# Layer two of a routed two-layer network: the second token halves of six experts with W2 held and h streamed

## The chip, the core and the metric

The kernel runs on one core of a Trainium2 chip. The core has five engines that each follow their own instruction queue: TensorE (PE in the profile; its weight loads are shown apart as PEld), VectorE (DVE), ScalarE (ACT), GpSimd (POOL) and SyncE (SP), which here only issues transfers. They wait for one another through semaphores. The metric is the device time of one execution in microseconds (us). Before the change three runs took 569.81, 570.81 and 574.17 us, a median of 570.81 us.

## The reference, cut to what matters

```
kv   = einsum('bhsd,bhse->bhde', k, v)            # 8 batches, 8 heads, 576 tokens, 64 wide
out  = einsum('bhsd,bhde->bhse', q, kv)
x    = (out / rms(out) * g_norm)  -> (8, 576, 512)
e    = expert of each token (argmax of logits, or the previous token's, by a local gate)
h    = max(x @ w1[e], 0)                          # 512 -> 1024
out  = softmax(logits)[e] * (h @ w2[e])           # 1024 -> 512, all in float32
```

There are 4608 tokens and 8 experts, and each token goes through one expert alone. With these inputs expert 0 has 455 tokens, and the others, sorted by load, have 720, 666, 605, 596, 588, 548 and 430.

## The kernel before, in words

The first part (the first 120 us or so) computes the attention part, writes the rows of x to a scratch tensor `xs` in DRAM and sorts the tokens into slots, expert by expert. Then expert 0 is computed, and after it the seven other experts one after the other, in order of their load: **ranks** 1 to 7, with room for WIDTHS = 720, 672, 608, 608, 592, 576 and 448 tokens. Rank 1's first matmul starts at 180.50 us of the profiled span; from there to the end is the part in which the change lies.

A rank is done in two token **halves**: `parts` (L1404) gives the first half 384 tokens (ranks 1 and 2) or 256, and the second half what is left: 336, 288, 352, 352, 336, 320 and 192. Each half has these stages:

- **Gathers.** The tokens' rows come from `xs` by indirect transfers that GpSimd issues: four for a block of 128 tokens, 128 quarter rows each (L785). `Block.scale` multiplies them by their gate on VectorE (L1339 to L1346), and `turn4` (L796) turns them, so that features lie on partitions: a 32x32 transpose on VectorE (L802), a copy on ScalarE (L806), a subtraction on VectorE (L807).
- **Layer one**, `first_wide` (L1053). Float32 precision is reached with two float32r parts of each number, a high one and a low one, and three matmuls for each product: high by high, low by high, high by low (`split_mm`, L960). W1 is the operand held in the array (stationary), and the tokens are streamed (moving), so a matmul streams as many columns as the half has tokens; there are 8 groups `f` of 128 hidden features x 4 pieces of the input x 3 = 96 matmuls. After each `f` ScalarE writes the high part of h (L1050) and VectorE the low part (L1051). Three PSUM banks take turns.
- **Layer two**, `Block.second` and `products` (L985 to L1017). Here each block of 128 tokens is done by itself: h is stationary, and W2 is moving, 512 columns: 8 x 3 = 24 matmuls of 512 columns for a block, whether it holds 128 tokens or 80. A last block of 32 or 64 tokens has its low parts put beside its high parts in the array, and takes 16 matmuls (`halves`, L1025 to L1040); layer one's `halved=True` prepares that (L1070). ScalarE copies the result from PSUM to the tile `ot` (L1013), and GpSimd issues one indirect transfer that scatters up to 128 whole rows of 2 KB to the output (L1016).

So second halves have three blocks, of 128+128+80, 128+128+32, 128+128+96, 128+128+96, 128+128+80 and 128+128+64 tokens: 72, 64, 72, 72, 72 and 64 matmuls of 512 columns.

The order of the instructions on PE, ACT, DVE and POOL in this part is the order of the code. Work for other engines is put between matmuls: `then` runs a step behind a group `f` of layer one, hooks run at an `f` of layer two, and `tick` (L1432) issues from two lists: `outs`, which is empty in the kernel before, and `todo`, the gathers for the half after the next. The weights of the next rank come in through SyncE, and `wsplit` splits them into high and low parts on ScalarE (L235, L238) and VectorE (L236, L239).

A function `second_turned` (L1367) stands in the file and is not called.

## Time and profile before

| What | us |
|---|---|
| three runs | 569.81, 570.81, 574.17 (median 570.81) |
| the profiled execution, its own time | 576.47 |
| its span, first to last instruction | 574.6 |
| mean granted TensorE clock in it | 0.992 of 2.4 GHz |
| PE busy | 548.0 (95%) |
| PEld, DVE, ACT, POOL busy | 481.5, 306.1, 238.5, 242.2 |

The profile is of one execution, 5.7 us above the median of the runs and 2.3 us above the slowest of them. "Busy" adds up the instructions of an engine; matmuls are pipelined, so one that starts every 0.23 us lasts 0.39 us in the rows, and the time a stage costs is read from the starts of its matmuls, not from their length. "issue" and "remote" behind an arrow stand for a wait that the profile can't put down to an instruction of another engine.

### The profile page before, as it was taken

Reading aid. Unit: us, or ns where it says so; the run is one execution under the profiler, and the core shown is the slowest. Engines: PE = TensorE matmul, PEld = TensorE weight load, DVE = VectorE, ACT = ScalarE, POOL = GpSimd, SP = SyncE. Lnnn points to the kernel's source line nnn. Section 1 sums busy time; section 2 is a strip of 40 time slices with the busy share of each in tenths; the row PEclk is TensorE's granted clock in tenths of the full one; section 3 lists DMA queues with packets and bytes.
Section 4 is the critical chain, followed back from the end, with each engine's and each line's share of the span. In section 5 each row is a group of like instructions: output and inputs, shape, how many; then the busy total and the mean of one; then the engine's idle time right before and its main releaser. Section 6 shows DMA issues by size and latency. Waiting matters only on the chain. (4 is left out here: it accounts for less than half of the span.)

```text
span 574.6 us, 11830 instructions
## 1 busy us (share of the span) xinstructions
PE 548.0 (95%) x4637; PEld 481.5 (84%) x4637; DVE 306.1 (53%) x638; ACT 238.5 (41%) x449; POOL 242.2 (42%) x305
## 2 busy tenths in 40 slices
PE   2999998989998999999989999999999999999996
PEld 2888887879877989798877998889897979898894
DVE  1125786669686724635435744474546554564610
ACT  1578886761254334331424341533433332434311
POOL 5234433251335736633352463366435744562001
PEclk9999998989999999999999999999999999999998
DMA  7999999970666345232441353445143533442010
GB/s 224 311 361 353 359 336 351 329 267 23 228 231 245 115 142 167 68 123 86 135 120 56 135 175 74 125 150 177 39 164 130 169 94 133 139 123 80 1 38 31
DMA packets 41296, 94.91 MB, mean 165 GB/s; under 512 B 7167, under 2 KB 7167, under 8 KB 41232
## 3 DMA queue, kind: packets, MB, share of 16 engines
q1 hardware_dynamic: 32032, 72.64, 37.2%
q0 software_dynamic: 7664, 21.41, 12.5%
q8 instruction: 38, 0.62, 0.5%
q10 hardware_dynamic: 1536, 0.02, 0.1%
q14 instruction: 26, 0.21, 0.1%
HBM read 73.85 MB, written 20.46 MB: 164 GB/s over the span
## 5 line engine op out<-in xcount | busy, mean ns | idle before, releaser
L785 POOL DMA_INDIRECT xr<-xs,gid x120 | 136.9, 1141 | 36.6 <-issue 35.4
L1051 DVE SCALAR_TENSOR_TENSOR hl<-ph,hh 128x512 fp32r<-128x512 f32 (+4 forms) x92 | 50.3, 548 | 126.9 <-ACT hh L1050 100.6
L1050 ACT ACTIVATE hh<-ph 128x512 fp32r<-128x512 f32 (+5 forms) x92 | 45.3, 496 | 143.8 <-PE ph L972 106.7
L1016 POOL DMA_INDIRECT out_dram<-ot,sidr x33 | 36.6, 1108 | 152.7 <-ACT ot L1013 90.7
L465 PE MATMUL po<-kvz,qT 128*64 128x146 f32 x512 | 45.6, 307 | 0.5 <-ACT kvz L434 0.4
L500 POOL TENSOR_TENSOR sq<-raw 128x576 f32<-128x576 f32 x16 | 20.4, 1276 | 55.0 <-ACT raw L469 38.0
L465 PEld LDWEIGHTS po<-kvz,qT 128*64 128x64 f32 x512 | 35.7, 145 | 6.3 <-issue 2.2
L1013 ACT COPY ot<-py 128x512 f32<-128x512 f32 (+2 forms) x33 | 19.2, 580 | 51.7 <-issue 31.7
L505 DVE TENSOR_REDUCE ms<-sq 128x9 f32<-128x576 f32 x32 | 23.1, 748 | 23.8 <-POOL sq L500 22.2
L380 PE MATMUL po<-vt,kt 64*64 64x64 f32 x1152 | 23.4, 233 | 10.7 <-DMA vt<-in_v_dram 10.7
L380 PEld LDWEIGHTS po<-vt,kt 64*64 64x64 f32 x1152 | 20.8, 145 | 14.2 <-issue 6.8
L469 ACT COPY raw<-po 128x876 f32<-128x876 f32 (+1 forms) x32 | 22.8, 715 | 13.8 <-PE po L465 13.6
L404 POOL COPY kvz<-kvp 64x128 f32<-64x128 f32 x64 | 20.3, 317 | 13.4 <-ACT kvp L384 8.7
L1346 DVE TENSOR_TENSOR xr<-xr,r 128x512 f32<-128x512 f32 x36 | 25.0, 696 | 1.2
L806 ACT CAST yh<-xT 128x512 fp32r<-128x512 f32 x17 | 10.6, 621 | 29.5 <-DVE xT L802 25.3
L802 DVE STREAM_TRANSPOSE xT<-xr 128x512 f32<-128x512 f32 x30 | 21.2, 708 | 0.6
L972 PE MATMUL py<-w_0h,hl 128*128 128x512 f32 (+2 forms) x54 | 21.3, 394 | 0.3 <-issue 0.3
L966 PE MATMUL py<-w_0h,hh 128*128 128x512 f32 (+2 forms) x54 | 21.3, 395 | 0.2 <-ACT ot L1013 0.2
L966 PE MATMUL py<-w_1h,hh 128*128 128x512 f32 (+2 forms) x54 | 21.4, 397 | 0.0
L971 PE MATMUL py<-w_0l,hh 128*128 128x512 f32 (+2 forms) x54 | 21.2, 392 | 0.0
L972 PE MATMUL py<-w_1h,hl 128*128 128x512 f32 (+2 forms) x54 | 21.1, 391 | 0.0
L971 PE MATMUL py<-w_1l,hh 128*128 128x512 f32 (+2 forms) x54 | 21.1, 390 | 0.0
(434 smaller groups left out, 1649.8 us busy)
## 6 DMA issues: line engine op xcount, KB each, us to landing
wst<-in_moe_w_dram SPq DMA_DIRECT2D x64, 512.0 KB
xs<-raw SPq DMA_DIRECT2D x36, 292.0 KB
kt<-in_k_dram SPq DMA_DIRECT2D x32, 288.0 KB
vt<-in_v_dram SPq DMA_DIRECT2D x32, 288.0 KB
qt<-in_q_dram SPq DMA_DIRECT2D x32, 288.0 KB
xr<-xs,gid POOLq DMA_INDIRECT x120
out_dram<-ot,sidr POOLq DMA_INDIRECT x36
xr<-xs,gidr POOLq DMA_INDIRECT x6
```

Of the source, the lines that this page charges most:

```text
L380: nc.tensor.matmul(pk[half(x ^ b), x, 0:D], ks[b][half(x), cd], vs[b][half(x), cd], start=(c == 0), stop=(c == C - 1))
L465: nc.tensor.matmul(po[half(b), x, o:o + n], lw[:, half(x)], kvb[:, z0:z0 + n], start=True, stop=True)
L469: nc.scalar.copy(cols[:, c0:c1].rearrange("p c (x e) -> p x c e", x=2), po[:, :, 0:(c1 - c0) * HW].rearrange("p x (c e) -> p x c e", e=HW))
L505: nc.vector.tensor_reduce(mss[g][:, :, 2 * n + x], sqs.pop((s, x)), axis=AX.X, op=ALU.add)
L785: i = nc.gpsimd.indirect_dma_start(out=xr[:, u * PW:(u + 1) * PW], out_offset=None, in_=xs.rearrange("t (q w) -> (t q) w", w=PW), in_offse ...
L966: mm = nc.tensor.matmul(ps, ah, bh, start=(first and i == 0), stop=False)
L971: nc.tensor.matmul(ps, ah, bl, start=False, stop=False)
L972: nc.tensor.matmul(ps, al, bh, start=False, stop=(last and i == n - 1))
L1016: return nc.gpsimd.indirect_dma_start(out=outf, out_offset=bass.IndirectOffsetOnAxis(ap=idx[0:m], axis=0), in_=ot[0:m], in_offset=None, bo ...
L1050: nc.scalar.activation(hh, ps, AF.Relu)
L1051: nc.vector.scalar_tensor_tensor(hl, ps[:, :, 0:nl], 0.0, hh[:, :, 0:nl].bitcast(F32), op0=ALU.max, op1=ALU.subtract)
L1346: nc.vector.tensor_mul(xv, xv, r4.unsqueeze(3).to_broadcast([P, NP, 2, D]))
```

## The change

In ranks 1 to 6 the second half's layer two is done by `second_turned`. For each of 4 groups `j` of 128 output features and each of 8 groups `f` of hidden features it holds a 128x128 piece of W2 and streams h, with as many columns as the half has tokens: 4 x 8 x 3 = 96 matmuls for all tokens of the half. VectorE then takes each of the 4 results out of PSUM with a 32x32 transpose into a quarter of one buffer `oq`, in which a partition holds, for a group `u` of 32 tokens, a quarter row of 128 features. One indirect transfer for each `u` scatters 128 quarter rows of 512 bytes, by the indices `sid4`, which are new. The scatters are put into `outs`, and `tick` issues three of them at a time, ahead of the gathers, in the next rank's first half; gathers then come two at a time in first halves and one in second halves.

What goes with it: W2's columns are put into another order when it is split, for ranks 1 to 6, so that the first halves, which still go block by block, read W2 in four runs of 128 columns and write `ot` in runs of 32 (`turned=True`); layer one of ranks 1 to 6 has no `halved` form; rank 6 has room for 560 tokens in the place of 576, so its second half has 304; `ot` has 2 buffers in the place of 3, and the turned tokens of expert 0's last blocks 1 in the place of 2; `by_quarter` computes `sid4` with some more small VectorE operations, and GpSimd writes one more constant, `spot`, at the start.

The transfers of SyncE stay as they were, in the same order. The changed order on the other engines, at three places:

PE, rank 3, from the end of layer one of the second half (`ph`, 352 tokens) to layer one of the next rank (256 tokens); `py` is layer two, `w_0` to `w_3` are tiles of W2 there, `h` and `l` at a name's end the high and low part. Before (the first seven of 72 matmuls in `py`):

```order
L972 MATMUL ph<-yh,w_7l 128x352
L966 MATMUL py<-w_0h,hh 128x512
L971 MATMUL py<-w_0l,hh 128x512
L972 MATMUL py<-w_0h,hl 128x512
L966 MATMUL py<-w_0h,hh 128x512
L971 MATMUL py<-w_0l,hh 128x512
L972 MATMUL py<-w_0h,hl 128x512
L966 MATMUL py<-w_1h,hh 128x512
```

And in the changed kernel:

```order
L987 MATMUL ph<-yh,w_7l 128x352
L981 MATMUL py<-hh,w_0h 128x352
L986 MATMUL py<-hl,w_0h 128x352
L987 MATMUL py<-hh,w_0l 128x352
L981 MATMUL py<-hh,w_0h 128x352
L986 MATMUL py<-hl,w_0h 128x352
```

72 matmuls of 512 columns have become 96 of 352, and all 8 groups of h are read by the first 24 of them, as they were by the first block's 24 before.

POOL, from the gathers for rank 3's second half on, through rank 3 and up to the scatters of its second half. Before (`xr` are gathers, `out_dram` scatters):

```order
L785 DMA xr<-xs,gid_88 128x146 x10
L1016 DMA out_dram<-ot,sidr 4608x512
L785 DMA xr<-xs,gid_88 128x146 x2
L1016 DMA out_dram<-ot,sidr 4608x512
L1040 DMA out_dram<-ot,sidr 4608x512
L785 DMA xr<-xs,gid_88 128x146 x6
L1016 DMA out_dram<-ot,sidr 4608x512
L785 DMA xr<-xs,gid_88 128x146 x2
L1016 DMA out_dram<-ot,sidr 4608x512
L785 DMA xr<-xs,gid_88 128x146 x10
```

And in the changed kernel:

```order
L800 DMA xr<-xs,gid_88 128x146 x12
L1380 DMA out_dram<-oq,sid_90 18432x128 x9
L800 DMA xr<-xs,gid_88 128x146 x6
L1031 DMA out_dram<-ot,sidr 4608x512
L800 DMA xr<-xs,gid_88 128x146 x2
L1031 DMA out_dram<-ot,sidr 4608x512
L800 DMA xr<-xs,gid_88 128x146 x12
L1380 DMA out_dram<-oq,sid_90 18432x128 x11
L800 DMA xr<-xs,gid_88 128x146 x4
```

Three scatters of whole rows have become 9 to 11 scatters of quarter rows, which stand in one piece ahead of the next rank's gathers.

DVE, rank 3, from the last low part of h in the second half to the next rank's first one (`xT`, `xl` are the next rank's tokens, `w_..l` weights to be split). Before:

```order
L1051 SCALAR_TENSOR_TENSOR hl<-ph,hh 128x352
L1339 TENSOR_TENSOR gs<-xr,oneh 128x28
...
L1346 TENSOR_TENSOR xr<-xr,r_4828 128x4x128
L802 STREAM_TRANSPOSE xT<-xr 128x4x4x32
L807 TENSOR_TENSOR xl<-xT,xh 128x4x128
L802 STREAM_TRANSPOSE xT<-xr 128x4x4x32
L807 TENSOR_TENSOR xl<-xT,xh 128x4x128
L239 SCALAR_TENSOR_TENSOR w_3l<-wst,gq,w_3h 128x1024
L236 TENSOR_TENSOR w_4l<-wst,w_4h 128x1024
L236 TENSOR_TENSOR w_5l<-wst,w_5h 128x1024
L1051 SCALAR_TENSOR_TENSOR hl<-ph,hh 128x2x256
```

And in the changed kernel:

```order
L817 STREAM_TRANSPOSE xT<-xr 128x4x4x32
L822 TENSOR_TENSOR xl<-xT,xh 128x4x128
L244 SCALAR_TENSOR_TENSOR w_3l<-wst,gq,w_3h 128x1024
L1407 STREAM_TRANSPOSE oq<-py 128x11x32
L817 STREAM_TRANSPOSE xT<-xr 128x4x4x32
L822 TENSOR_TENSOR xl<-xT,xh 128x4x128
L241 TENSOR_TENSOR w_4l<-wst,w_4h 128x1024
L1407 STREAM_TRANSPOSE oq<-py 128x11x32
L241 TENSOR_TENSOR w_5l<-wst,w_5h 128x1024
L1407 STREAM_TRANSPOSE oq<-py 128x11x32 x2
L1066 SCALAR_TENSOR_TENSOR hl<-ph,hh 128x2x256
```

Four transposes out of PSUM have come into the queue; what else stands there is as it was, with the two turns a little further apart.

The diff, cut to its core:

```diff
@@ -56,7 +56,7 @@
-    WIDTHS = (720, 672, 608, 608, 592, 576, 448)
+    WIDTHS = (720, 672, 608, 608, 592, 560, 448)
     NR = E - 1
@@ -110,6 +110,7 @@
     quart = const.tile([P, 2], F32, name="quart")
+    sid4 = const.tile([P, NP, NR * KBM - KBM], I32, name="sid4")
     own4 = const.tile([P, NP], F32, name="own4")
@@ -127,6 +128,10 @@
+    spot = const.tile([P, 1], F32, name="spot")
+    for n in range(NP):
+        nc.gpsimd.iota(spot[n * QD:(n + 1) * QD], pattern=[[0, 1]], base=0, channel_multiplier=1,
+                       allow_small_or_imprecise_dtypes=True)
     def floor_div(dst, src, n, tmp):
@@ -252,7 +257,7 @@
         hi, lo = (wtile(pool, nm + x) for x in "hl")
-        low_ = split_w(hi, lo, t, i, e > 1, False)
+        low_ = split_w(hi, lo, t, i, e > 1, 0 < e < E - 1)
         wt[e, i] = (hi, lo)
@@ -654,13 +659,23 @@
-        n = NR * KBM - KBM
+        n = NR * KBM
         pq4 = rbank[:, 128:128 + NP * n].rearrange("p (u n) -> p u n", n=n)
         for u in range(NP):
-            nc.tensor.matmul(pq4[:, u], sel[0][:, u], trs[0][:, KBM:], start=True, stop=True)
+            nc.tensor.matmul(pq4[:, u], sel[0][:, u], trs[0], start=True, stop=True)
         t = sm.tile([P, NP, n], F32, name="q4", tag="co")
         nc.vector.tensor_scalar(t, pq4, float(NP), quart[:, 1:2], op0=ALU.mult, op1=ALU.add)
-        nc.vector.tensor_scalar(gid4, t, quart[:, 0:1], None, op0=ALU.max)
+        nc.vector.tensor_scalar(gid4, t[:, :, KBM:], quart[:, 0:1], None, op0=ALU.max)
+        m = n - KBM
+        none = sm.tile([P, NP, m], F32, name="none", tag="lo")
+        nc.vector.tensor_scalar(none, pq4[:, :, 0:m], 0.0, None, op0=ALU.is_equal)
+        for i, w_ in enumerate(WIDTHS[:-1]):
+            if w_ % QD:
+                cell = none[:, w_ % P // QD, i * KBM + w_ // P:i * KBM + w_ // P + 1]
+                nc.vector.scalar_tensor_tensor(cell, spot, float(w_ % QD), cell,
+                                               op0=ALU.is_ge, op1=ALU.max)
+        nc.vector.scalar_tensor_tensor(sid4, none, float(NP * (NT + 1)), t[:, :, 0:m],
+                                       op0=ALU.mult, op1=ALU.add)
@@ -1117,7 +1132,7 @@
     def xtiles(pool, n, nm):
-        return tuple(pool.tile([P, ND, n], F32R, name=nm + x, bufs=2 if nm == "t" else 1)
+        return tuple(pool.tile([P, ND, n], F32R, name=nm + x, bufs=1)
                      for x in "hl")
@@ -1138,7 +1153,6 @@
         fourth.append(gather(xtile0(), cidx(gidx, 3)))
-        fourth.extend(xtiles(z, P, "t"))
@@ -1193,6 +1207,7 @@
                     assert "y" in done
+                    fourth.extend(xtiles(z, P, "t"))
                     turn(*fourth, 0, ps_t)
@@ -1353,18 +1368,24 @@
             return (products if last else second)(z, w, hh, hl, t0, None, cidx(sidr, self.c), ps_y, hooks,
-                                                   m=self.m, turned=False)
+                                                   m=self.m, turned=self.r < E - 1)
...
-    def brought(ys, x, bl):
-
-        m = -(-bl.m // QD) * QD
-        ot = z.tile([P, DM], F32, name="ot", bufs=ot_bufs[0])
-        fetch(ot[0:m], ys[x * P:x * P + m])
-        return ot
-
-    def second_turned(w, hh, hl, n, lot, hooks, sites):
+    out4 = out.rearrange("b s (q w) -> (b s q) w", w=P)
+    scattered = []
+
+    def scatter(oq, u, c):
+
+        i = nc.gpsimd.indirect_dma_start(
+            out=out4, out_offset=bass.IndirectOffsetOnAxis(
+                ap=sid4[:, u % NP, c + u // NP:c + u // NP + 1], axis=0),
+            in_=oq[:, u], in_offset=None, bounds_check=NT * NP - 1, oob_is_err=False)
+        for j in scattered:
+            tc.declare_no_dep(i.ins, j.ins.name, reason="a token is in one slot alone")
+        scattered.append(i)
+
+    def second_turned(w, hh, hl, n, c, hooks):
@@ -1385,21 +1406,7 @@
                                 py[:, 0:nu * QD].rearrange("p (u k) -> p u k", k=QD))
-        ys = dram.tile([HM, DM], F32, name="ys", bufs=2)
-        for q_ in range(NP):
-            fetch(ys[0:nu * QD, q_ * P:(q_ + 1) * P].rearrange("(u k) w -> k u w", k=QD),
-                  oq[q_ * QD:(q_ + 1) * QD, 0:nu])
-        ots = []
-
-        def scatter(x):
-            bl = lot[x]
-            nc.gpsimd.indirect_dma_start(
-                out=outf, out_offset=bass.IndirectOffsetOnAxis(ap=cidx(sidr, bl.c)[0:bl.m], axis=0),
-                in_=ots[x][0:bl.m], in_offset=None, bounds_check=NT - 1, oob_is_err=False)
-
-        outs.extend(lambda: None for _ in range(sites))
-        outs.append(lambda: ots.extend(brought(ys, x, bl) for x, bl in enumerate(lot)))
-        outs.extend(lambda x=x: scatter(x) for x in range(len(lot)))
+        outs.extend(lambda u=u: scatter(oq, u, c) for u in range(nu))
@@ -1426,14 +1433,17 @@
     z = wpool("z")
-    ot_bufs[0] = 3
+    ot_bufs[0] = 2
     todo = []
...
-        for lot in (outs, todo):
+        lot, n = (outs, 3) if outs else (todo, rate[0])
+        for _ in range(n):
             if lot:
                 lot.pop(0)()
+
+    rate = [1]
@@ -1463,6 +1473,7 @@
             todo = [what for bl in ma for what in bl.gathers()]
+            rate[0] = 2
             own = [lambda j=j: wsplit(*j)
@@ -1474,7 +1485,7 @@
             first_wide({i: wt[r, i] for i in range(NW1)}, hh, hl, *xt, n=na, then=then, each=tick,
-                       halved=True)
+                       halved=r == E - 1)
             w = {i: wt[r, i] for i in range(NW1 + NW2)}
@@ -1502,17 +1513,16 @@
             todo = [what for bl in mb_ for what in bl.gathers()]
+            rate[0] = 1
             first_wide(w, hh, hl, *yt, n=nb, then=then, each=tick,
-                       halved=True)
+                       halved=r == E - 1)
             xt = xtiles(xp, HM, "x")
             turns = [lambda x=x, bl=bl: bl.turn(*xt, x * P) for x, bl in enumerate(ma)]
-            pairs_ = list(enumerate(lb))
-            for left_, (x, bl) in zip(range(len(lb), 0, -1), pairs_ if ma else reversed(pairs_)):
+            if r < E - 1:
+                second_turned(w, hh, hl, nb, lb[0].c, spread(turns, nxt))
+            for x, bl in reversed(list(enumerate(lb)) if r == E - 1 else []):
+                left_ = x + 1
                 hooks = []
-                for f in (1, 4):
-                    two(hooks, f, turns)
-                if nxt:
-                    hooks.append((7, nxt.pop(0)))
                 end = bl.second(w, hh, hl, x * P, with_ticks(hooks), not ma and left_ == 1)
...
                 tick()
```

## Rows read from the trace of the kernel before

**Rows 1.** The page: busy share of PE, and its granted clock in 40 slices.

```profile
PE 548.0 (95%) x4637; PEld 481.5 (84%) x4637; DVE 306.1 (53%) x638; ACT 238.5 (41%) x449; POOL 242.2 (42%) x305
...
PEclk9999998989999999999999999999999999999998
```

**Rows 2.** Waits of PE from 255 to 575 us: total, times, longest.

```profile
PE ph L966 <- DVE hh L1070: 1.2, 1, 1.2
PE py L972 <- DVE hl L1051: 0.7, 1, 0.7
PE ph L971 <- DVE yl L807: 0.3, 1, 0.3
```

**Rows 3.** Stretches: length, then PE, PEld, DVE, ACT, POOL busy; clock, DMA.

```profile
216.04:230.77 14.73, 14.73 (x97) 14.73 (x96) 7.64 (x17) 5.83 (x10) 9.45 (x8) 1.00 0.52 160
230.77:247.36 16.59, 16.59 (x74) 12.57 (x73) 8.78 (x14) 5.28 (x8) 9.69 (x8) 1.00 0.30 75
281.00:295.28 14.28, 13.03 (x97) 12.83 (x96) 5.25 (x13) 5.14 (x9) 9.51 (x9) 1.00 0.62 188
295.28:311.43 16.15, 15.33 (x67) 10.86 (x65) 8.76 (x20) 4.83 (x8) 4.88 (x5) 1.00 0.12 30
333.63:349.10 15.47, 15.47 (x97) 15.47 (x96) 5.49 (x9) 5.34 (x9) 11.05 (x11) 1.00 0.63 188
349.10:366.37 17.27, 17.06 (x73) 12.65 (x73) 9.78 (x17) 6.08 (x9) 5.84 (x6) 1.00 0.25 67
388.76:403.97 15.21, 15.21 (x97) 15.20 (x96) 6.44 (x12) 5.92 (x10) 10.02 (x10) 1.00 0.58 176
403.97:420.57 16.60, 16.60 (x75) 12.90 (x74) 8.87 (x14) 5.71 (x8) 6.85 (x7) 1.00 0.25 76
443.17:458.58 15.41, 15.10 (x97) 14.87 (x97) 8.55 (x15) 6.72 (x11) 12.36 (x11) 1.00 0.61 180
458.58:475.20 16.62, 16.62 (x74) 12.56 (x73) 8.69 (x13) 5.70 (x8) 7.42 (x7) 1.00 0.35 99
497.42:511.58 14.16, 14.16 (x98) 14.05 (x96) 8.06 (x21) 6.00 (x11) 11.41 (x10) 1.00 0.57 174
511.58:526.13 14.55, 14.55 (x66) 12.02 (x65) 8.81 (x14) 5.69 (x8) 3.65 (x4) 1.00 0.25 71
```

**Rows 4.** Timeline of PE at rank 2's layer one: start, length, what.

```profile
281.00 0.30 PE L966 MATMUL ph<-yh,w_0h 128*128 128x288 f32 x1
281.13 0.29 PE L971 MATMUL ph<-yl,w_0h 128*128 128x288 f32 x1
```

**Rows 5.** DVE from 225 to 575 us, grouped: busy and mean ns.

```profile
L802 DVE STREAM_TRANSPOSE xT<-xr 128x512 f32<-128x512 f32 x30 | 21.2, 708 | 0.6
...
L1051 DVE SCALAR_TENSOR_TENSOR hl<-ph,hh 128x352 fp32r<-128x352 f32 x16 | 8.3, 523 | 22.4 <-issue 15.2 <-ACT hh L1050 7.2
```

**Rows 6.** The page: ScalarE copies out of PSUM, contiguous and interleaved.

```profile
L1013 ACT COPY ot<-py 128x512 f32<-128x512 f32 (+2 forms) x33 | 19.2, 580 | 51.7 <-issue 31.7
...
L469 ACT COPY raw<-po 128x876 f32<-128x876 f32 (+1 forms) x32 | 22.8, 715 | 13.8 <-PE po L465 13.6
```

**Rows 7.** POOL from 240 to 576 us, grouped: busy and mean ns.

```profile
L785 POOL DMA_INDIRECT xr<-xs,gid x98 | 107.8, 1100 | 29.9 <-issue 29.0 <-DVE hl L1051 0.3 <-DMA out_dram<-ot,sidr 0.3
L1016 POOL DMA_INDIRECT out_dram<-ot,sidr x29 | 31.5, 1087 | 136.4 <-ACT ot L1013 82.2 <-issue 23.0 <-DMA out_dram<-ot,sidr 13.1
```

**Rows 8.** Timeline of POOL, two gathers in a row.

```profile
292.85 1.00 POOL L785 DMA_INDIRECT xr<-xs,gid  x1 [0.30 <-issue]
294.15 1.00 POOL L785 DMA_INDIRECT xr<-xs,gid  x1 [0.30 <-issue]
```

**Rows 9.** Timelines of ACT and DVE, late parts of h, ranks 2 and 4.

```profile
298.95 0.71 ACT L1050 ACTIVATE hh<-ph 128x288 fp32r<-128x288 f32 x2 [3.86 <-remote]
301.07 0.42 DVE L1051 SCALAR_TENSOR_TENSOR hl<-ph,hh 128x256 fp32r<-128x256 f32 x1
407.31 0.53 DVE L1051 SCALAR_TENSOR_TENSOR hl<-ph,hh 128x352 fp32r<-128x352 f32 x1 [2.55 <-issue]
```

## The prediction, as it was written before the run

> **What bounds the kernel now.** The page comes first: PE is busy 95% of the span and its granted clock stands at the upper level, 2.4 GHz, in nearly all slices, while VectorE, ScalarE and GpSimd are busy for 53, 41 and 42% [rows 1]. The chain of waits does not help here, since most of it is "issue"; the table of waits of PE does: in the 320 us from 255 us on PE waits for other engines for little more than 2 us [rows 2]. So in this part time is matmul time, and a change is worth what it takes from PE's stream, as long as nothing new makes PE wait. The stretches [rows 3] cut this stream at the first matmul of each stage: the rows come in pairs, layer one and layer two of the second half, for ranks 1 to 6 in turn. PE is busy for the whole of most of them.
>
> **What a matmul costs.** Two neighbours of 288 columns start 0.13 us apart [rows 4], and layer one's 96 matmuls at 352 columns take 15.21 us [rows 3], 0.1584 us each. 288 columns at 2.4 GHz are 0.120 us and 352 are 0.1467, so each matmul carries some 12 to 14 ns beyond its columns. A 512-column matmul of layer two takes 16.60 / 72 = 0.2306 us (rank 4), or 14.55 / 64 = 0.2273 us (rank 6), where its columns are 0.2133.
>
> **The main term.** The new layer two is, in shape, a copy of layer one of the same half: 96 matmuls, W held, n columns streamed. So layer one's own stretch gives its price, and the gain is the difference within each pair of rows 3, both taken without waits:
>
> - Rank 1: 16.59 before. Layer one's 96 matmuls at 336 columns take 14.73. The first group of columns is 352 wide in 12 of the 96, 12 x 16 / 2.4 ns = 0.08. After: 14.81, gain 1.78.
> - Rank 2: 64 matmuls at rank 6's 0.2273 are 14.55; 96 at 0.1333 are 12.80. Gain 1.75.
> - Ranks 3 and 4: 16.60 to 15.21, gain 1.39 each.
> - Rank 5: 16.62 to 14.81, gain 1.81.
> - Rank 6: 14.55 before; 14.16 at 320 columns less 96 x 6.7 ns for 16 columns fewer, and 0.08 more for the first group, is 13.60 at 304. Gain 0.95, and layer one of this half gains 0.56 in the same way.
> - Layer one of ranks 1 and 5 has the wider first group too: 0.08 lost, twice.
>
> The sum is a gain of 9.47 us. The columns saved alone are worth more: some 23,500 in layer two, 9.8 us at 2.4 GHz, and 160 more matmuls at 13 ns take 2.1 back; rank 6's layer one gives the rest.
>
> A rule can be set against the row here. The Trainium skill, "TensorE: Matmul & The Clock Gate", section "Back-to-back issue gap", puts the gap between isolated matmuls at N/2.4 plus about 2.5 ns. By that the extra matmuls would cost 0.4 us and the gain would be some 11 us. These traces show 12 to 14 ns instead, and the sum stays with the rows.
>
> **What lies beside PE.**
>
> - VectorE gets 24 transposes out of PSUM of 288 to 352 columns. The nearest rows are 523 ns for a 352-column operation out of PSUM and 708 ns for a 512-column transpose [rows 5], so about 0.53 us each and 2.1 us in a second half. In rank 4's layer two VectorE is busy for 8.87 of 16.60 us; it becomes 11.0 of 15.2. Each has a PSUM buffer of its own to run in, and PE comes back to that buffer one group `j`, some 3.7 us, later. Hidden. The few operations for `sid4` and the constant `spot` are short, on engines that wait there anyway: nothing.
> - ScalarE loses three copies of 580 ns in each of these halves.
> - Runs of 32 in the place of whole rows: ScalarE's copy of 876 columns with interleaved output takes 715 ns against 580 for 512 contiguous ones [rows 6], no price for the pattern; the 512-column transpose reads and writes in runs of 32 and takes what plain operations take. So splitting W2 and writing `ot` cost what they did.
> - GpSimd: 9 to 11 scatters for 3. One takes 1.09 us, as a gather of quarter rows does [rows 7], and two gathers in a row start 1.30 us apart [rows 8]. With rank 3's 11 scatters, 8 gathers for rank 4's first half, 2 scatters of whole rows and 12 gathers, rank 4 holds 33 issues, 42.9 us; its PE time would be 22.39 (from 366.37 to 388.76) + 15.21 + 15.21 = 52.8. The gathers that are needed first stand behind the 11 scatters: issued by 11 + 4 + 1 + 4 issues, 26 us after the rank's start, while their use comes in group 6 of the next layer one, at about 22.4 + 6 x 1.9 = 34 us. Some 8 us of room, for landing too. Hidden.
> - The reordered W2 is streamed in four runs of 128 columns in the first halves: 14 blocks x 24 = 336 matmuls. No row shows such an operand on PE. Nothing points to a gain, so the lower end is 0; the upper end is one matmul's own extra, 13 ns, for each of three further runs, 39 ns or 13 us in all. I take 0, by ScalarE's rows, where interleaving is free.
>
> **Waits at the seams.** Layer two used to read the last part of h after 22 of its 0.23 us matmuls, 5.1 us after its start; now it comes there after 22 x 0.158 = 3.5 us (352 columns) or 2.9 (288). ScalarE's last parts of h are sometimes late, by waits that the profile names "remote": in rank 4 the low part is ready at 407.31 + 0.53 = 407.84, 3.87 us after layer two's start, and in rank 2 at 301.49, 6.2 us after it [rows 9]. If these delays come again in the same places, rank 4 loses 0.4 us and rank 2 loses 3.3 where it loses 1.6 now: a gain of 9.47 becomes 1.78 + 0.05 + 1.39 + 0.99 + 1.81 + 0.95 + 0.56 - 0.16 = 7.4. If none of today's waits returns (1.60 and 14.28 - 12.80 = 1.48 in rank 2, 17.27 - 16.60 = 0.67 in rank 3, 15.41 - 14.73 = 0.68 in rank 5's layer one), it is 13.9. I take the middle way, 9.5.
>
> **From the profile to the runs.** The profiled execution took 576.5 us, which would give 567.0; it stands 5.7 above the median of the runs. The stages lie inside it and should be as long in the other runs, so from the median 570.8 the forecast is 561.3.
>
> **The rivals.**
>
> 1. *The gain is eaten at the seams.* PE reaches h earlier in every second half, and ScalarE's delays are 3 to 5 us long. For it: two of six halves had one within reach [rows 9], and VectorE's queue between two groups `j` is fuller. Against it: PE hardly waits today. If four more halves lost 1 to 1.5 us on top of the 7.4 case, 2 or 3 us of gain are left: about 568.
> 2. *The streamed runs cost.* At 39 ns for each of 336 matmuls 13.1 us are lost: 570.8 - 9.5 + 13.1 = 574.4. It decides from 28 ns on. Against it: ScalarE's and VectorE's rows; on PE no row speaks.
> 3. *GpSimd becomes the bound: slower.* Rank 4 has room for 11 scatters of (52.8 - 22 x 1.30) / 11 = 2.2 us. Were each to cost 3.0 us, start to start, rank 4 would last 61.6 in the place of 52.8, and by the same count ranks 2, 3, 5 and 6 would last 3.7, 3.0, 9.4 and 7.0 us more: 32 us in all, 593. For it: they are many, and stand ahead of the gathers in one queue. Against it: 98 gathers of the same 128 pieces average 1.10 us [rows 7] with VectorE busy beside them, and the issue order shows no scatter of this kind waiting for the one before. The Trainium skill, "SBUF — State Buffer", section "SBUF: two separate sides", would make such issues wait whenever a VectorE operation holds the port that it shares with GpSimd; the gathers' rows show no such stretch.
>
> That the change does not do what it says is ruled out by the order of the instructions: 96 matmuls and 9 to 11 scatters stand there.
>
> **The numbers.** Chances: the forecast 0.66 (its own range 557 to 565: gains of 13.9 and 7.4, and the runs' spread), the first rival 0.19, the second 0.05, the third 0.06, something unforeseen on the slow side 0.04. A measurement of this kernel tells about 1%, 5.7 us, from no change: below 565.1 is faster. Nearly all of the forecast and a tenth of the first rival lie there: 0.67. Within 1% lie the rest of these, and most of the second rival: 0.22. Slower: 0.11. The range reaches from 556 to 571, over the first rival, and leaves out the other two.
>
> **What would show it.** Right: layer two of ranks 1 to 6 with 96 matmuls 0.133 to 0.16 us apart, as in layer one of the same half; first halves as long as before (22.2 to 22.6 us in ranks 3 to 5); GpSimd's scatters 1.3 us apart. Wrong: 512-column matmuls of the first halves over 0.25 us apart (rival 2); scatters over 2 us apart and VectorE's scaling waiting for gathers (rival 3); waits of PE for `hh` or `hl` at the first group `j` (rival 1).

## The result: 1.2 to 1.7% faster

The changed kernel took 565.65 us (median of 567.41, 560.20, 563.89 and 568.47), the kernel before 571.74 in four runs: a ratio of 0.9875 [0.9829, 0.9921]. Two later measurements put it at 0.9842 [0.9797, 0.9888], 563.38 us, and 0.9835 [0.9801, 0.987], 562.83 us, each against the kernel before on the same chip (571.77 and 571.89). So the medians gain 6.1, 8.4 and 9.1 us. The forecast was 561.3 us, 0.983 of the 570.81 it started from.

The page after, in the lines that answer [rows 1], and those of the new operations (line, engine, operation, count | busy us, mean ns | idle time before it, by what):

```profile
PE 536.9 (95%) x4797; PEld 493.9 (87%) x4797; DVE 314.4 (56%) x649; ACT 229.5 (41%) x431; POOL 293.6 (52%) x354
...
L1380 POOL DMA_INDIRECT out_dram<-oq,sid x63 | 67.9, 1077 | 56.8 <-DVE oq L1407 39.4
...
L1407 DVE STREAM_TRANSPOSE oq<-py 128x352 f32<-128x352 f32 (+2 forms) x24 | 12.6, 526 | 17.6 <-PE py L987 17.4
```

160 more matmuls, 11 us less of PE; GpSimd is the engine that pays, 242 to 294 us. The stretches after, in the order of [rows 3] (layer one, layer two of the second half, ranks 1 to 6):

```profile
220.28:235.08 14.80, 14.80 (x98) 14.80 (x96) 7.64 (x17) 5.83 (x10) 9.68 (x8) 1.00 0.49 157
235.08:249.88 14.80, 14.80 (x98) 14.80 (x97) 10.00 (x17) 4.22 (x6) 6.56 (x6) 1.00 0.29 71
283.49:296.29 12.80, 12.80 (x98) 12.80 (x97) 5.95 (x11) 5.54 (x10) 6.94 (x6) 1.00 0.52 165
296.29:309.86 13.57, 13.17 (x99) 12.79 (x98) 8.56 (x16) 3.55 (x5) 8.63 (x8) 1.00 0.34 72
332.06:347.42 15.36, 15.36 (x98) 15.36 (x96) 6.78 (x14) 5.92 (x10) 10.88 (x10) 1.00 0.59 176
347.42:362.89 15.47, 15.47 (x98) 15.47 (x98) 9.89 (x16) 4.66 (x6) 6.45 (x7) 1.00 0.30 89
385.24:400.61 15.37, 15.37 (x98) 15.37 (x97) 6.68 (x13) 5.92 (x10) 12.02 (x12) 1.00 0.69 186
400.61:415.97 15.36, 15.36 (x97) 15.36 (x97) 9.92 (x16) 4.66 (x6) 7.74 (x7) 1.00 0.33 89
438.40:453.19 14.79, 14.79 (x97) 14.79 (x96) 6.50 (x13) 5.83 (x10) 11.74 (x11) 1.00 0.65 182
453.19:467.99 14.80, 14.80 (x98) 14.80 (x97) 9.83 (x16) 4.65 (x6) 8.73 (x8) 1.00 0.34 91
490.15:503.68 13.53, 13.53 (x98) 13.52 (x96) 6.31 (x14) 5.65 (x10) 10.53 (x10) 1.00 0.71 200
503.68:517.51 13.83, 13.61 (x99) 13.37 (x98) 9.76 (x16) 4.62 (x6) 5.93 (x4) 1.00 0.25 69
```

Each layer two now lasts as long as the layer one above it, but for 0.8 us in rank 2 and 0.3 in rank 6, where PE is not busy all the time. The table of waits of PE from 225 to 560 us, against [rows 2], has one line, and it says why:

```profile
PE py L981 <- DVE oq L1407: 0.6, 2, 0.4
```

**Where the span hides the gain.** The two profiled spans differ by 9.0 us (574.6, 565.6). From rank 1's first matmul to the last of `py` it is 388.9 before (180.50 to 569.43) and 375.3 after (185.04 to 560.37), 13.6 less; 4.5 of that is lost ahead of rank 1, in a part that the change hardly touches. These 4.5 us, and 5.5 of the 13.6, are chance, as the next section shows; 8.05 are the change.

### The profile page after: what moved, and what is told of

It is laid out like the page before. It is cut to its first block, busy times and chain, and to the rows that moved or that the text cites. A ratio compares the mean times of both kernels' runs of the same rounds, so it can differ in the third digit from the quotient of the medians.

```text
span 565.6 us, 12192 instructions
## 1 busy us (share of the span) xinstructions
PE 536.9 (95%) x4797; PEld 493.9 (87%) x4797; DVE 314.4 (56%) x649; ACT 229.5 (41%) x431; POOL 293.6 (52%) x354
## 5 line engine op out<-in xcount | busy, mean ns | idle before, releaser
L1065 ACT ACTIVATE hh<-ph 128x512 fp32r<-128x512 f32 (+6 forms) x92 | 45.6, 495 | 158.5 <-PE ph L987 158.5
L1066 DVE SCALAR_TENSOR_TENSOR hl<-ph,hh 128x512 fp32r<-128x512 f32 (+7 forms) x92 | 51.0, 555 | 95.4 <-ACT hh L1065 91.9
L1380 POOL DMA_INDIRECT out_dram<-oq,sid x63 | 67.9, 1077 | 56.8 <-DVE oq L1407 39.4
L1031 POOL DMA_INDIRECT out_dram<-ot,sidr x17 | 18.7, 1100 | 39.8 <-issue 12.7
L1407 DVE STREAM_TRANSPOSE oq<-py 128x352 f32<-128x352 f32 (+2 forms) x24 | 12.6, 526 | 17.6 <-PE py L987 17.4
L449 PE MATMUL pq<-ident,qt 128*128 128x128 f32 x128 | 18.9, 289 | 2.5 <-DMA qt<-in_q_dram 2.2
L821 ACT CAST xh<-xT 128x512 fp32r<-128x512 f32 x13 | 8.1, 620 | 31.3 <-DVE xT L817 31.3
L450 ACT COPY qT<-pq 128x512 f32<-128x512 f32 x32 | 17.6, 588 | 5.7 <-PE pq L449 5.0
L449 PEld LDWEIGHTS pq<-ident,qt 128*128 128x128 f32 x128 | 14.5, 146 | 4.5 <-DMA qt<-in_q_dram 3.5
L822 DVE TENSOR_TENSOR yl<-xT,yh 128x512 fp32r<-128x512 f32 x17 | 11.8, 692 | 11.7 <-ACT yh L821 11.7
```

Source lines behind the costliest of these rows:

```text
L449: nc.tensor.transpose(pq[:, w], qts[s, b][:, w * P:(w + 1) * P], ident)
L1065: nc.scalar.activation(hh, ps, AF.Relu)
L1066: nc.vector.scalar_tensor_tensor(hl, ps[:, :, 0:nl], 0.0, hh[:, :, 0:nl].bitcast(F32), op0=ALU.max, op1=ALU.subtract)
L1380: i = nc.gpsimd.indirect_dma_start(out=out4, out_offset=bass.IndirectOffsetOnAxis(ap=sid4[:, u % NP, c + u // NP:c + u // NP + 1], axis=0) ...
```

## The experiments

**before_again and after_again: both kernels unaltered, on one chip.**

Expected: 

> The kernel before, unchanged, profiled a second time. Theory (columns): the part from rank 1's first matmul to the last one, 388.9 us in the first profile, holds about 4 us of waits that are chance (ScalarE's late parts of h in ranks 2, 3 and 5), so it comes between 385 and 390 again; the start of rank 1, at 180.50 us, moves by some us from execution to execution because the part before it waits for loads. Rival (the change makes the first part longer): rank 1 starts at 180.5 within 1 us again. On ScalarE's 'remote' delays: if they belong to the old form of the halves, they come again in the same ranks; if they are chance, elsewhere or not at all.

> The changed kernel, unchanged, profiled and timed again. Theory (columns): the part from rank 1's first matmul to the last is 375 to 378 us again, and rank 1's start lies anywhere between 180 and 186 us; the ratio to before is 0.980 to 0.988 (a gain of 9.5 us and up to 2 of waits). Rival (the change makes the first part longer): rank 1 starts at 185 within 1 us again, and the ratio stays at 0.987 to 0.990.

Measured: 571.23 us (one run) and 563.38. Rank 1 starts at 180.77 and 180.71 us; over the profiles of this study it starts between 178 and 186 us, the changed kernel alone at 180.7, 182.9 and 185.0. The rank part is 383.42 (to 564.19) and 375.37 (to 556.08): the change is worth **8.05 us**. That is under the 385 to 390 expected for the kernel before: 5.5 us of the first profile were chance, not about 4. They stand in six stages of ranks 2, 3 and 5, with ScalarE's late relus ("remote" in [rows 9]), which do not come again here; the changed kernel's rank part came out at 375.33, 375.37 and 375.39 in three profiles.

Of the 8.05, layer two of the second halves gives 95.55 - 87.86 = 7.69, their layer one 87.05 - 86.65 = 0.40, and the rest nothing: layer one of the first halves of ranks 1, 2, 5 and 7 moves by 0.3 to 0.4 us, two each way. By ranks, layer two gains 1.78, 1.16, 0.98, 1.23, 1.82 and 0.72. Ranks 2 and 3 of before_again, for the rows of [rows 3] that held chance waits:

```profile
293.66:308.41 14.75, 14.75 (x67) 11.16 (x65) 7.51 (x14) 4.62 (x7) 7.25 (x7) 1.00 0.26 73
346.08:362.53 16.45, 16.45 (x74) 12.88 (x73) 8.64 (x13) 5.72 (x8) 5.66 (x6) 1.00 0.34 96
```

**e1_blocks: second halves block by block again, all else as changed.** Rank 2's third block, of 32 tokens, then takes 24 matmuls, not 16, and so does rank 6's, which has room for 48 at the new width. The edit, cut:

```
-        if m in HALF:
+        if m in HALF and not turned:
...
-            if r < E - 1:
-                second_turned(w, hh, hl, nb, lb[0].c, spread(turns, nxt))
...
+            pairs_ = list(enumerate(lb))
+            for left_, (x, bl) in zip(range(len(lb), 0, -1), pairs_ if ma else reversed(pairs_)):
...
```

Expected: 

> The changed kernel with one part undone: the second halves of ranks 1 to 6 go block by block again (h held, 512 columns of W2 streamed, 24 matmuls a block, whole rows scattered by three transfers); W2's order, the first halves' streamed runs, rank 6's width of 560, the index tables and the buffers stay as changed. Theory (columns): layer two of these halves is 72 x 0.2306 = 16.6 us each again, in sum 13 us more than in the changed kernel (1.8, 3.8, 1.2, 1.2, 1.8 and 3.0 in ranks 1 to 6), layer one as in the changed kernel: time 13 us above the changed kernel, 2 to 4 us above the kernel before, whose 16-matmul blocks of 32 and 64 tokens are missing here. Rival (half of the gain is what goes with it: order of VectorE and ScalarE, fewer copies): at most 7 us above the changed kernel.

Measured: 576.53 us, ratio 1.0071 [1.0044, 1.0098]: 13.2 more than after_again, where 13 were expected, and 4.8 more than the kernel before, where 2 to 4 were. Layer two takes 99.59 us over the six, as expected, but that is only 11.7 more than in the changed kernel, with PE busy throughout. The other 1.4 us of the medians are not placed. The profiled execution, 5.2 us above its median, has 1.7 more in rank 1's first stage, whose first 12 matmuls start 0.32 us apart (granted clock 0.61), ahead of anything that the edit touches; so the total fits the 13 in part by luck. Layer two of ranks 1 and 2:

```profile
237.81:254.46 16.65, 16.65 (x75) 12.58 (x73) 8.77 (x14) 5.28 (x8) 8.15 (x7) 1.00 0.25 72
300.57:317.26 16.69, 16.69 (x75) 11.62 (x73) 7.37 (x13) 4.62 (x7) 8.13 (x8) 1.00 0.25 75
```

Layer one of the second halves stays at 86.64 us. So what goes with the held W2 does not bring the gain, but for the 0.57 us that rank 6's width gives in its layer one. Rank 5's and rank 6's first halves read W2 in its new order in both kernels, and their layer two stays at 11.12 and 10.90 us for 48 matmuls, 11.06 and 10.91 before.

**e2_twice: every scatter of a second half issued twice**, the second time to a spare tensor.

```
...
- outs.extend(lambda u=u: scatter(oq, u, c) for u in range(nu))
+ outs.extend(lambda u=u: (scatter(oq, u, c), scatter2(oq, u, c)) for u in range(nu))
```

Expected: 

> The changed kernel with every scatter of quarter rows issued a second time, to a scratch tensor that nobody reads: 18 to 22 issues of 1.3 us at the start of ranks 2 to 7 in the place of 9 to 11. The prediction gave GpSimd about 8 us of room before the gathers for the next first half come too late. By that count 11 further issues take 14.3 us: rank 3 (9 further) loses 2 to 4 us, ranks 4, 5 and 6 about 6 to 9 us each, ranks 2 and 7 nothing: 18 to 30 us slower than the changed kernel, with VectorE's scaling of the gathered rows waiting for transfers late in layer one. Rival (there is far more room, or the gathers are not what is needed first): under 3 us slower. Rival (PE is already held back by the scatters as they are): the loss shows in all ranks and reaches 60 us.

Measured: 602.31 us, 1.0526 [1.0464, 1.0588], 39 over after_again, more than the 18 to 30 expected. Rank 2's layer one, and layer two of ranks 4, 5 and 6, lose 9.0, 11.5, 7.2 and 10.6 us; nothing was expected of rank 2, and rank 3, of which 2 to 4 were, loses nothing. Of the waits of all engines (total, times, longest), four lines:

```profile
DVE gs L1354 <- DMA xr<-xs,gid: 26.5, 7, 5.2
...
PE py L981 <- DVE oq L1420: 16.4, 4, 5.7
...
ACT ot L1025 <- DMA out_dram<-ot,sidr: 14.6, 1, 14.6
...
PE ph L981 <- DVE hl L1066: 7.4, 1, 7.4
```

GpSimd bounds ranks 4 to 6 as rival 3 had it: gathers stand behind scatters in its queue, VectorE's scaling waits for them, the transposes of `oq` stand behind the scaling, and PE waits for the buffer that they free. Rank 2 shows a second way: the third `ot` of its first half waits for the first one's scatter, since `ot` has two buffers. So one scatter per `u` has room, two have not. The granted clock falls with the waits: 0.84 to 0.92 in these four stretches, 1.00 in all those of the changed kernel.

**e3_banks: a second pair of PSUM buffers for the results.** The third and fourth result go to the pool of `pt`.

```
- py = ps_y.tile([P, DM], F32, name="py")
+ py = ps_y.tile([P, DM], F32, name="py") if j < 2 else \
+     ps_t.tile([P, ND, P], F32, name="pt", tag="pt").rearrange("p a b -> p (a b)")
```

Expected: 

> The changed kernel, with the third and fourth result of each second half's layer two in PSUM buffers of the pool that the token transposes of expert 0 used, so that each of the four has one of its own. In both profiles of the changed kernel TensorE waits for a transpose out of PSUM in ranks 2 and 6 (layer two 13.59 and 13.83 us, against 12.80 and 13.52 of layer one of the same halves). Theory (too few buffers at the narrow halves): both waits go, 0.8 and 0.3 us, layer two of ranks 2 and 6 comes to 12.8 and 13.5; the time falls by 1 us, which the runs can't tell from nothing. Rival (VectorE itself is behind): the wait moves to the next layer one, and nothing is gained.

Measured: 599.76 us, 36 more than the changed kernel, where 1 us less was expected. ScalarE's instructions are those of the changed kernel in the same order, and its relus (the L1065 operations that write h) were late. Rank 2's first half, ScalarE in e3_banks:

```profile
254.49 0.49 ACT L1065 ACTIVATE hh<-ph 128x384 fp32r<-128x384 f32 x1 [1.63 <-issue]
259.67 0.49 ACT L1065 ACTIVATE hh<-ph 128x384 fp32r<-128x384 f32 x1 [3.75 <-PE ph L987]
265.38 0.49 ACT L1065 ACTIVATE hh<-ph 128x384 fp32r<-128x384 f32 x1 [5.21 <-remote]
275.94 1.25 ACT L1065 ACTIVATE hh<-ph 128x384 fp32r<-128x384 f32 x3 [10.08 <-remote]
```

In the changed kernel (after_third, below) these relus come 2.12 us apart. The next two runs set the edit and the changed kernel side by side on one chip.

**after_third and e3_again: the changed kernel and e3_banks, on another chip.**

Expected: 

> The changed kernel itself, unaltered, beside e3_again on one chip. In e3_banks, e4_wide and e5_late, which shared a chip, ScalarE began its relus 3 to 15 us after the product that they read had ended, though by the program they wait for that product alone, and TensorE then ran at 1.2 GHz for stretches. Theory A (the chip or the moment does it, to any kernel with the held-W2 form): this kernel is 562 to 568 us on a chip where e3_again is within 3 us of it, and 590 to 605 us on a chip where e3_again is slow too. Theory B (the result bank moved in e3_banks does it): this kernel is 562 to 568 us and e3_again 590 to 604 us.

> The kernel of e3_banks again: of the changed kernel, the third and fourth result of each second half written to the other two-buffer pool of PSUM. Theory A (the late relus come from the chip or the moment): its time less that of the changed kernel in this call is -1 us, the two waits of 0.4 to 0.6 us before a transpose that ranks 2 and 6 lose, give or take 2 us, and its ScalarE shows no idle time before a relu that the profile can't explain where the changed kernel shows none. Theory B (the bank does it): 590 to 604 us again with 30 us of such idle time, whatever the changed kernel takes.

Measured: 562.83 and 563.15 us, ratios 0.9835 [0.9801, 0.987] and 0.9845 [0.9814, 0.9877]. Theory A holds: the same kernel lacks the 36 us here, and e4_wide and e5_late, without the second pair of buffers, had late relus beside e3_banks, so the buffers alone do not bring them. The stages now tell the bank apart; rank 2's and rank 6's layer two, first the changed kernel, then e3_again:

```profile
294.13:307.72 13.59, 13.18 (x98) 12.80 (x97) 8.57 (x16) 3.56 (x5) 8.64 (x8) 1.00 0.36 77
501.55:515.38 13.83, 13.60 (x98) 13.36 (x97) 9.78 (x16) 4.62 (x6) 4.30 (x4) 1.00 0.27 67
```

```profile
289.35:302.09 12.74, 12.74 (x99) 12.74 (x97) 8.56 (x16) 3.56 (x5) 8.63 (x8) 1.00 0.35 77
495.91:509.25 13.34, 13.34 (x99) 13.34 (x97) 9.78 (x16) 4.62 (x6) 4.31 (x4) 1.00 0.27 73
```

0.85 and 0.49 us come back, PE is busy throughout in these two stages, and the rank part is 374.03 against 375.39. The medians, which the first part's chance moves by some us, do not show 1.4 us.

**e5_late, e5_again, e6_late_blocks: six idle copies on ScalarE** ahead of the last parts of h in the second halves of ranks 1 to 6, in the changed kernel (e5) and in e1_blocks (e6).

```
+ def idle():
+     for _ in range(6):
+         nc.scalar.copy(spent, spent)
...
+                        halved=r == E - 1, pre=idle if r < E - 1 else None)
```

Expected: 

> The changed kernel with six spare copies of 128x512 on ScalarE, some 0.55 us each, ahead of the last part of h in layer one of each second half of ranks 1 to 6: h's last part comes about 3.3 us later. In the changed kernel's profile it is complete 1.2 us after layer two's start and read 2.9 to 3.5 us after it. Theory (the seam has got shorter): the cover of 1.7 to 2.3 us is passed by 1 to 1.6 us in each half, seen as waits of TensorE in the first group of layer two: 5 to 9 us slower than the changed kernel. Rival (order on ScalarE and VectorE leaves the same room as before): under 2 us slower.

> The form with blocks again (h held, 512 columns of W2 streamed) and the same six spare copies on ScalarE. Here h's last part is read 22 x 0.23 = 5.1 us after layer two's start. Theory (the seam has got shorter by the change): 1.2 + 3.3 = 4.5 us is still in time, so under 2 us slower than the form with blocks alone (576.5 us). Rival (the copies cost what they cost in either form): as much slower as the changed kernel becomes by them.

> The kernel of e5_late again (six copies, 3.87 us of ScalarE in one block, ahead of the last parts of h in the second halves of ranks 1 to 6), on a chip without the late relus. In the changed kernel rank 4's last hl is ready 1.2 us after layer two's start and read 3.5 us after it, 2.3 us of room. Theory A (the seams bind once ScalarE is 3.9 us late, as the prediction's step on the seams has it): each second half loses 1 to 1.7 us in layer two, 6 to 10 us in all, 569 to 573. Theory B (there is more room than that): 563 to 565. If the chip brings the late relus again: over 590.

Measured: 619.31 us (e5_late), 579.98 us (e6_late_blocks) and 635.07 us (e5_again). The two runs of e5 had the late relus from rank 2's first half on, and their totals say nothing of the seams. Rank 1 lies ahead of that, and its layer two took 16.47 and 16.48 us in the two, for 14.81; rank 2's took 15.88 and 15.89, for 13.59. On VectorE, rank 1, layer two from 233.78 us on, e5_again:

```profile
236.74 0.51 DVE L1066 SCALAR_TENSOR_TENSOR hl<-ph,hh 128x336 fp32r<-128x336 f32 x1 [2.31 <-ACT hh L1065]
...
240.80 1.23 DVE L241 TENSOR_TENSOR w_2l<-wst,w_2h 128x1024 fp32r<-128x1024 f32 x1 [0.26 <-issue]
241.94 0.54 DVE L1409 STREAM_TRANSPOSE oq<-py 128x352 f32<-128x352 f32 x1
```

The last `hl` is ready 3.5 us after layer two's start, just in time for PE. But the first transpose stands behind it in VectorE's queue, with a scaling, a turn and a weight split between the two, and PE, back at that buffer, waits for it:

```profile
PE py L981 <- DVE oq L1409: 1.0, 1, 1.0
```

So the loss is 1.7 us in rank 1 and 2.3 in rank 2, where theory A had 1 to 1.7, and not where it said: PE waits mostly for the result's buffer (1.1 us in rank 1; in rank 2 some 2.2, where the changed kernel has 0.8), and h costs only 0.2 and 0.7. In e6, with blocks, the copies cost nothing in layer two of ranks 1 to 4: 16.65, 16.69, 16.43 and 16.61 us, against 16.65, 16.69, 16.42 and 16.61 in e1. (The ratios, 1.009 [1.0041, 1.0139] and 1.0071 [1.0044, 1.0098], come from two chips.) There PE reads the last part of h 22 x 0.23 = 5.1 us after the start, and ScalarE, not VectorE, empties the result.

**e4_wide, e4_again: all second halves 384 wide.**

```
- WIDTHS = (720, 672, 608, 608, 592, 560, 448)
+ WIDTHS = (768, 768, 640, 640, 640, 640, 448)
```

Expected: 

> The changed kernel with one size changed: room for 768, 768, 640, 640, 640 and 640 tokens in ranks 1 to 6, so that every second half streams 384 columns (same tokens, more empty slots). Theory (only the columns that blocks pad are saved): layer two of each half takes 96 x 0.1734 = 16.65 us, what three blocks take, 16.6: the held-W2 form is worth nothing at 384 columns. Against the changed kernel layer two takes 12 us more (99.9 for 87.9) and layer one 13 us more (99.9 for 86.6): 588 us. Rival (the form saves by itself, by fewer copies and waits): layer two under 16.3 us, time under 584.

> The kernel of e4_wide again (widths 768, 768, 640, 640, 640, 640: 384 columns in each second half), on a chip without the late relus. From its stages: layer two of the six second halves at 16.67 to 16.83 instead of 87.86 in all, +12.6; layer one at 16.64 instead of 14.80, 12.80, 15.36, 15.37, 14.79 and 13.52, +13.2 in all: 25.8 more than the changed kernel, 588 to 590. If what was seen there beyond that belongs to the kernel and not to the chip: 620 or more.

Measured: 630.96 and 645.04 us, both with late relus throughout; no total is to be read from them. In e4_wide, stages without them give the price: layer two at 384 columns takes 16.67 to 16.83 us in the six ranks (and 16.67 in ranks 3 and 6 of e4_again), and by blocks of 512 columns it took 16.60 [rows 3]. Ranks 2 and 3:

```profile
314.55:331.38 16.83, 16.83 (x97) 16.83 (x97) 8.75 (x15) 3.64 (x5) 2.30 (x2) 1.00 0.20 65
375.20:391.87 16.67, 16.67 (x98) 16.67 (x98) 9.93 (x16) 4.69 (x6) 5.83 (x5) 1.00 0.29 83
```

The gain comes from the width that was streamed for nothing, and is gone at three full blocks.

**What stays open: the late relus.** Five runs had them (e3_banks, e4_wide and e5_late on one chip, e4_again and e5_again on another), e6_late_blocks beside these had a few, and the other six runs and the first profile of after none or next to none. They are not bound to the held W2: the kernel before had them in its first profile, from the sixth and seventh relu of rank 2's first half on (2.59 and 5.20 us of idle time). In the five runs they come at a place in ScalarE's program, not at a time: the fourth, fifth and sixth relu of rank 2's first half start after 3.0 to 4.5, 4.5 to 5.9 and 9.4 to 10.8 us of idle time in all five, where 0.7 to 1.6 is usual; then they come again in layer one of later second halves. The product that such a relu waits for had ended; the profile calls the rest "remote" and "issue". Loads of instructions do not mark them: the traces have 16 KB ones some 20 us apart, and a late relu starts anywhere from 2.5 to 33 us after the last of them. After them TensorE's clock is low: in e3_banks 512-column matmuls start 0.42 to 0.43 us apart, at a granted clock of 0.50 (1.2 GHz).

```profile
276.52 0.63 PE L987 MATMUL py<-w_3h,hl 128*128 128x512 f32 x1
276.95 0.63 PE L981 MATMUL py<-w_3h,hh 128*128 128x512 f32 x1
```

On those two chips the kernel before had medians of 575.28 and 579.49, 3.5 and 7.7 us over the 571.8 of a quiet one, e6_late_blocks 579.98, and e3_banks, which is the changed kernel but for a buffer, 599.76. That the changed kernel suffers there as e3_banks did is likely, but not shown: it was not run there. If so, it is slower than before there, as e3_banks was (1.0377 [1.0286, 1.0468]), and the gain above is that of quiet chips. The cause was not found.

## Why the prediction was right, point by point

- **The bound and the main term.** Right in mechanism: 9.47 us were forecast for layer two and rank 6's width, 8.05 measured without the chance waits. Ranks 1 and 5 gain 1.78 and 1.82 (1.78 and 1.81 forecast); e1_blocks takes 11.7 of layer two away. The prediction's own count by columns does not come to its sum: 9.8 less 2.1, and layer one's 0.56 less 0.16, are 8.1, not 9.47. That this lies near the 8.05 is luck: it takes 13 ns beyond the columns for every matmul, where its rows had 14 to 17 at 512 columns and 12 to 14 at the narrow ones, and it knows no buffer waits. By the same count the 2.5 ns give 9.8 us, not "some 11".
- **The term that was mis-sized: "PE comes back to that buffer one group `j`, some 3.7 us, later. Hidden."** The transposes do take 0.53 us (526 ns). But VectorE's queue is in order, and ahead of the transpose stand steps that wait for ScalarE. Rank 2 in the changed kernel, VectorE:

```profile
302.59 0.67 DVE L817 STREAM_TRANSPOSE xT<-xr 128x512 f32<-128x512 f32 x1
303.95 0.69 DVE L822 TENSOR_TENSOR xl<-xT,xh 128x512 fp32r<-128x512 f32 x1 [0.69 <-ACT xh L821]
304.89 1.23 DVE L241 TENSOR_TENSOR w_1l<-wst,w_1h 128x1024 fp32r<-128x1024 f32 x1 [0.26 <-ACT w_1h L240]
306.04 0.84 DVE L1407 STREAM_TRANSPOSE oq<-py 128x288 f32<-128x288 f32 x2
```

  Two transposes are due by then; PE starts the last matmul of its group at 305.88 and the first of the next at 306.57, after the first of the two, where 0.13 us is usual. At 288 columns a group lasts 24 x 0.133 = 3.2 us, not 3.7. The prediction compared VectorE's busy time with the stretch and left out the order of its queue. Rank 2 is 0.79 us over its forecast of 12.80, rank 6 0.23 over 13.60; e3_again takes back 0.85 and 0.49.
- **Columns.** 352 columns cost 0.1600 to 0.1611 us a matmul, in layer one too. 0.1584 was taken from rank 4 alone, and rank 3's 15.47 in the same rows passed over: 0.26 us in rank 3, 0.15 in rank 4. With the buffer waits these are the 1.43 us by which layer two is over its forecast; nearly all that the gain lacks.
- **The extra of a matmul.** The Trainium skill, "TensorE: Matmul & The Clock Gate", section "Back-to-back issue gap", puts the gap between isolated matmuls at N/2.4 plus about 2.5 ns. This stream, with a weight load for each matmul, does not agree: 12.80 / 96 - 288 / 2400 leaves 13 ns, and 15.47 / 96 - 352 / 2400 leaves 14.
- **Rival 2, the streamed runs:** refuted. 48 matmuls of 512 columns take 10.90, 11.09 and 11.12 us in the first halves of ranks 3 to 5 after, 10.90, 11.08 and 11.06 in before_again.
- **Rival 3, GpSimd:** the price was right in the mean, 1.08 us, and most start 1.28 to 1.30 us apart; it does not decide at 1.3 us a scatter and does at 2.6 (e2_twice). In the rows after it idles for 8.21 us in rank 3's layer two, waiting for the first `oq`:

```profile
354.70 1.00 POOL L800 DMA_INDIRECT xr<-xs,gid  x1 [0.30 <-issue]
363.92 1.01 POOL L1380 DMA_INDIRECT out_dram<-oq,sid  x1 [8.21 <-DVE oq L1407]
365.23 1.00 POOL L1380 DMA_INDIRECT out_dram<-oq,sid  x1 [0.30 <-issue]
```

  But "the gathers' rows show no such stretch" was misread: the mean of 1.10 us hides them. Where an issue starts while VectorE runs an operation on two operands from SBUF (a weight split, a scaling, the subtraction of a turn), it lasts until that operation is over, and 0.9 us more. GpSimd and VectorE in the changed kernel, rank 4's layer two:

```profile
404.23 0.99 POOL L800 DMA_INDIRECT xr<-xs,gid  x1 [0.30 <-issue]
405.53 2.05 POOL L800 DMA_INDIRECT xr<-xs,gid  x1 [0.30 <-issue]
```

```profile
405.42 1.28 DVE L244 SCALAR_TENSOR_TENSOR w_7l<-wst,gq,w_7h 128x1024 fp32r<-128x1024 f32 x1 [0.36 <-ACT w_7h L243]
```

  From 240 us on, 69 of the 176 indirect issues in that profile start so, and 63 of them end 0.84 to 0.98 us after VectorE's operation. The other 107 take 0.92 to 1.04 us. In the kernel before it is 39 of 42, so the rows to read it from were there. No wait of PE in that profile comes of it, but it is part of what a scatter costs.

- **Rival 1, the seams:** the table of waits shows none of PE for h in the changed kernel. The room is real but small, and what uses it up is VectorE's queue ahead of the transposes (e5_again), not h itself.
- **From the profile to the runs.** "The stages lie inside it and should be as long in the other runs" was wrong by the 5.5 us of chance waits in the profile of before. The main term was taken from waitless rows, so it did not suffer. The bounds of 7.4 and 13.9 did: they count waits that the median of the runs, from which they are subtracted, seems not to have held (571.23 us in before_again without them), so 9.5 was no middle between two likely ends. The forecast is 1.5 to 2.1 us below the two later medians, 4.4 below the first, of which the smaller gain explains 1.4; the profiled one of the first four runs starts rank 1 some 4 us later than after_again.

## What to carry to other kernels

Hold the weights and stream the tokens where the last block of tokens is short: the price is read from a stage that already has this form, and the gain is the columns that were streamed for nothing. Whoever then empties the result must be early in its queue: look at what stands ahead of it and waits for a third engine, not at its busy time, and give the result a buffer more. Repeat both kernels before explaining a few microseconds: here the same program's first part moved by 4 us and its waits by 5.5.

## What the runs showed of the hardware

- An indirect transfer of 128 rows holds GpSimd for about 1.0 us plus 0.3, whether the rows are quarter rows of `oq` (mean 1077 ns) or whole ones (1087 ns [rows 7]). One that starts beside a VectorE operation on two SBUF operands ends some 0.9 us after that operation (63 of 69 in the changed kernel; the longest took 2.05 us).
- A 32x32 transpose of 352 columns out of PSUM takes VectorE 0.54 us, two of 288 columns 0.84.
- The same program was 599.8 us on one chip and 563.2 on another, while the kernel before moved by 3.4 (575.28, 571.89). A form can be worth 1.5% and still be one that is easily disturbed.
